# Channel-mix pieces drawn from a queue, centring on ScalarE and a reordered set-up in a fused RWKV-attention and channel-mix kernel

## The chip, the cores and the metric

The kernel runs on one core of one Trainium2 chip. The metric is the device time of one execution in microseconds (us); the median of several runs is quoted. The profile's span leaves out start and end, and is 1.8 to 2.1 us shorter than the time of the same execution in these runs.

## The reference, cut to what matters

Four sequences of 768 positions with 8 heads of 48 go through a linear-attention recurrence, then through a normalised two-layer channel mix with a residual.

```python
for t in range(S):                                   # per batch and head
    y[:, :, t] = r_t @ (state + (u * k_t) ⊗ v_t)
    state = w * state + k_t ⊗ v_t
x  = y as (4, 768, 384)
xn = (x - mean(x)) / sqrt(var(x) + 1e-6) * g_ln
out = x + max(xn @ w_ch1, 0) @ w_ch2                 # 384 -> 1536 -> 384
```

The kernel cuts the 3072 rows into 24 tiles of 128, six a sequence. Within a tile the recurrence becomes matrix products; from tile to tile a state Z is carried.

## The kernel before: the parts that matter

One pass of the main loop, a slot, does the attention of tile s and channel-mix work of earlier tiles. Each engine has its own stream of instructions, in the order of the program. A "piece" is one call of up or down; the bank o is the one buffer into which all down pieces write.

```python
def transposes(i):     # TensorE: 8 transposes into PSUM tr;  ScalarE: trs <- tr;  VectorE: q
def scores(i):         # TensorE: at, s;  VectorE: A, Z;  ScalarE: cc;  GpSimd: Vb
def values(i):
    ...                                             # TensorE: y
    nc.vector.tensor_tensor(out=x[:], in0=y[:, :C], in1=cc_t[i]..., op=ALU.add)
    nc.vector.bn_stats(out=stats[:], in_=x[:])
    nc.vector.bn_aggr(out=mv[:, i % GT, :], in_=stats[:])
    nc.vector.tensor_scalar(out=xn[:], in0=x[:], scalar1=mv[:, i % GT, 0:1],
                            scalar2=None, op0=ALU.subtract)
    ...                                             # every second tile: root on ScalarE, 1/x on VectorE
def ln_transposes(i):  # TensorE: 3 transposes of xn;  ScalarE: xT
def up(g, m):          # TensorE: 6 matmuls;  ScalarE: hT = relu(hp)
def down(i, m):        # TensorE: 4 matmuls into the one bank o;  after the third: VectorE ot, store

for s in range(NT + DN0):        # NT = 24, UP0 = 3, DN0 = 5: fixed delays
    if att: transposes(s)
    ...                          # load(s + 3) on GpSimd's queue
    up_slot(s, 0); down_slot(s, 0)
    if att: scores(s); scale(s + 1)
    up_slot(s, 1)
    ln_transposes(s - 1)
    down_slot(s, 1)
    if att: values(s)
    up_slot(s, 2); down_slot(s, 2)
```

In the set-up, load(0) and tiny transfers are issued ahead of w1 (2.36 MB, three transfers), and ScalarE multiplies w1 by g before it does anything for tile 0.

## Time and profile before

| before | |
|---|---|
| time | 182.42 us, median of 3 (182.04 to 183.57) |
| span, granted clock of the profiled execution (183.27 us) | 181.2 us, 0.991 |
| first x of tiles 1, 10, 23 | 24.42, 77.84, 157.31 us |

x is the first thing VectorE makes of a finished tile, so the starts of x(1), x(10) and x(23) cut the span into head, early slots, late slots and tail. The next lines are the busy times in the last three of these. Columns: stretch, its length, then busy us (and instructions) of TensorE, its weight loads, VectorE, ScalarE, GpSimd, then the clock, the DMA share and GB/s.

```profile
24.42:77.84 53.42, 47.60 (x559) 36.14 (x560) 42.77 (x92) 28.25 (x56) 31.87 (x37) 0.97 1.15 78
77.84:157.31 79.47, 75.41 (x888) 56.11 (x886) 64.21 (x132) 42.58 (x84) 36.46 (x43) 1.00 0.82 71
157.31:181.20 23.89, 17.82 (x127) 11.93 (x124) 5.41 (x11) 6.41 (x12) 0.00 (x0) 1.00 0.14 50
```

The late slots have TensorE busy for 95% (75.41 of 79.47). There is little room there; the head and the tail have more.

### The profile page before, as it was taken

To read this page: it belongs to the slowest core of one execution; us is meant where nothing else is said; L and a number is where in the kernel's file an instruction comes from. 1 tells how busy PE (TensorE), PEld (TensorE's weight loads), DVE (VectorE), ACT (ScalarE), POOL (GpSimd) and SP (SyncE) were. 2 spreads that over 40 slices of the span, in tenths; PEclk is the share of its full clock that TensorE was granted. 3 is DMA by queue.
4 is the path that set the end of the run, shared out by engine and by line. 5 is a ranking of instruction groups with operands and counts; after the bars stand their busy time and mean duration, and the time that the engine had idled before them with its cause. 6 is when DMAs were issued, how large, how long until landed. Compare 5 with 4: busy or idle time off the path is not lost.

```text
span 181.2 us, 4089 instructions
## 1 busy us (share of the span) xinstructions
PE 148.7 (82%) x1646; PEld 110.1 (61%) x1646; DVE 125.7 (69%) x278; ACT 87.3 (48%) x162; POOL 85.9 (47%) x105
## 2 busy tenths in 40 slices
PE   0323558969998999999989999999899999989871
PEld 0212347757676677667666866776677767767640
DVE  0843989876798797878888877878797879621211
ACT  2085262465545453654546455637455555454300
POOL 7946776754773475357536733764471101100000
PEclk9999999988999999999999999999999999999999
DMA  5999999999889968998999799699967110111121
GB/s 21 244 340 141 184 175 79 63 67 65 43 83 97 96 48 79 109 52 84 89 109 56 75 89 111 37 87 99 93 51 77 47 45 0 47 43 45 43 90 43
DMA packets 81971, 15.61 MB, mean 86 GB/s; under 512 B 76960, under 2 KB 81568, under 8 KB 81952
## 3 DMA queue, kind: packets, MB, share of 16 engines
q0 software_dynamic: 76432, 8.26, 80.0%
q1 hardware_dynamic: 5520, 7.09, 11.2%
q8 instruction: 13, 0.21, 0.5%
q14 instruction: 6, 0.05, 0.1%
HBM read 18.88 MB, written 4.72 MB: 130 GB/s over the span
## 4 chain that ended last, share of the span: by engine, by line
PE 47%; DVE 33%; issue 8%; DMA 5%; ACT 4%; SPq 2%; DVEq 0%
PE o L355 20%; PE hp L337 11%; DVE ot L364 8%; DVE stats L302 7%; DVE x L298 7%; DMA w_f<-in_moe_w_ch_dram 5%; PE at L203 5%; DVE xn L308 3%; DVE A L246 3%; DVE mv L306 2%; DVE Z L260 2%; ACT trs L190 2%; PE y L288 2%; PE s L215 2%; PE tr L327 2%
## 5 line engine op out<-in xcount | busy, mean ns | idle before, releaser
L355 PE MATMUL o<-w_sb,hT 128*128 128x384 bf16 x288 | 57.8, 325 | 8.0 <-DVE ot L364 7.7
L337 PE MATMUL hp<-xT,w_sb 128*128 128x256 bf16 x432 | 60.5, 277 | 0.0
L344 ACT ACTIVATE hT<-hp 128x512 bf16<-128x512 f32 x72 | 42.8, 597 | 25.4 <-PE hp L337 25.4
L255 POOL TENSOR_TENSOR Vb<-vv,cc 128x384 bf16<-128x384 bf16 x24 | 19.8, 826 | 66.5 <-ACT cc L253 66.5
L337 PEld LDWEIGHTS <-w_sb 128*128 128x128 bf16 x432 | 38.8, 99 | 5.1
L355 PEld LDWEIGHTS <-hT 128*128 128x128 bf16 x288 | 27.2, 97 | 23.0 <-issue 12.2
L246 DVE TENSOR_TENSOR A<-at,mask 128x512 bf16<-128x512 f32 x48 | 30.9, 685 | 9.5 <-PE at L203 9.2
L190 ACT COPY trs<-tr 128x1024 bf16<-128x1024 bf16 x24 | 24.2, 1006 | 9.1 <-PE tr L188 9.1
L364 DVE SCALAR_TENSOR_TENSOR ot<-o,rs,x 128x384 f32<-128x384 f32 x24 | 14.4, 602 | 15.1 <-PE o L355 15.1
L71 POOL DMA_DIRECT2D rk<-in_k_dram x24 | 22.6, 944 | 0.8 <-POOLq L432 0.8
L72 POOL DMA_DIRECT2D rk<-in_r_dram x24 | 21.3, 889 | 3.0 <-DMA vv<-in_v_dram 3.0
L73 POOL DMA_DIRECT2D vv<-in_v_dram x24 | 21.8, 907 | 0.0
L192 DVE TENSOR_TENSOR q<-trs 128x512 bf16<-128x512 bf16 x24 | 10.2, 425 | 14.9 <-ACT trs L190 14.8
L188 PE MATMUL tr<-ident,sc 128*128 128x128 bf16 x192 | 16.5, 236 | 4.1 <-DVE sc L180 4.1
L188 PEld LDWEIGHTS <-sc 128*128 128x128 bf16 x192 | 13.8, 106 | 7.6 <-DVE sc L180 5.1
L203 PE MATMUL at<-trs 48*128 48x128 bf16 x192 | 10.2, 229 | 8.5 <-ACT trs L190 8.5
L298 DVE TENSOR_TENSOR x<-y,Vb 128x384 f32<-128x384 f32 x24 | 13.3, 554 | 5.1 <-PE y L288 5.1
L203 PEld LDWEIGHTS <-trs 48*128 48x128 bf16 x192 | 5.8, 98 | 15.9 <-ACT trs L190 13.1
L308 DVE TENSOR_SCALAR xn<-x,mv 128x384 bf16<-128x384 f32 x24 | 14.1, 586 | 0.9
L253 ACT COPY cc<-s 128x8 f32<-128x8 f32 x24 | 4.0, 166 | 21.9 <-PE s L235 21.9
L302 DVE BATCH_NORM_STATS2 stats<-x 128x6 f32<-128x384 f32 x24 | 13.5, 560 | 0.8
L180 DVE TENSOR_TENSOR sc<-rk,F 128x768 bf16<-128x768 bf16 x24 | 13.4, 558 | 0.0
(49 smaller groups left out, 127.5 us busy)
## 6 DMA issues: line engine op xcount, KB each, us to landing
out_dram<-ot SPq DMA_DIRECT2D x24, 192.0 KB, 2.6
rk<-in_k_dram POOLq DMA_DIRECT2D x24, 96.0 KB, 3.3
rk<-in_r_dram POOLq DMA_DIRECT2D x24, 96.0 KB, 4.0
vv<-in_v_dram POOLq DMA_DIRECT2D x24, 96.0 KB, 3.9
w_f<-in_moe_w_ch_dram SPq DMA_DIRECT2D x3, 768.0 KB, 7.5
w_sb<-in_moe_w_ch_dram POOLq DMA_DIRECT2D x1, 1152.0 KB, 10.0
w_p<-in_w_dram SPq DMA_DIRECT2D x2, 0.8 KB, 2.0
u_p<-in_u_dram SPq DMA_DIRECT2D x2, 0.8 KB, 3.1
```

Of the source, the lines that this page charges most:

```text
L71: nc.gpsimd.dma_start(out=rk[:, 1], in_=k[b, :, s0 : s0 + L, :].rearrange("h t d -> t h d"))
L73: nc.gpsimd.dma_start(out=vv[:], in_=v[b, :, s0 : s0 + L, :].rearrange("h t d -> t h d"))
L188: nc.tensor.transpose(out=tp[:, j, :], in_=sc[:, j, :], identity=ident[:])
L190: nc.scalar.copy(out=tr[:], in_=tp[:].rearrange("p (a q) t -> p a q t", a=2))
L203: nc.tensor.matmul(out=at[:, par, p, :], lhsT=tr[p0 : p0 + D, 1, p, :], rhs=tr[p0 : p0 + D, 0, p, :], start=True, stop=True,)
L246: nc.vector.tensor_tensor(out=A[:, par], in0=at[:, par], in1=mask[:].unsqueeze(1).to_broadcast([P, HP, P]), op=ALU.mult,)
L298: nc.vector.tensor_tensor(out=x[:], in0=y[:, :C], in1=cc_t[i][:].rearrange("p h d -> p (h d)"), op=ALU.add)
L302: nc.vector.bn_stats(out=stats[:], in_=x[:])
L337: nc.tensor.matmul(out=hp[:, f, :], lhsT=w1_sb[:, kc, fk * P : (fk + 1) * P], rhs=xT_t[g][:, kc, :], start=(kc == 0), stop=(kc == CK - 1),)
L344: nc.scalar.activation(out=hT_t[g][:, 2 * m : 2 * m + 2, :], in_=hp[:], func=ACT.Relu)
L355: nc.tensor.matmul(out=o[:, :C], lhsT=hT_t[g][:, fk, j * P : (j + 1) * P], rhs=w2_sb[:, fk, :], start=(fk == 0), stop=(fk == FK - 1),)
L364: nc.vector.scalar_tensor_tensor(out=ot[:], in0=o[:, :C], scalar=mv_t[g][:, j : j + 1], in1=x_t[i][:], op0=ALU.mult, op1=ALU.add,)
```

## The change

Its intent: no slot without channel-mix work if there is any, and no bare wait for the o bank; less on VectorE; nothing of w1 in tile 0's way on ScalarE. Pieces wait in a queue, and fill(n) emits up to n of them. Centring on ScalarE gives mean - x, so w1 is scaled by -g. The core of the diff:

```diff
-            nc.sync.dma_start(                      # w_p, u_p, and g_sb alike
+            nc.scalar.dma_start(
-    load(0)                                         # now behind make_identity
...                                                  # T chain: F2 in two halves; small constants on GpSimd
-        nc.scalar.activation(out=w1_sb[:, kc, :], in_=w1_f[:, kc, :], func=ACT.Copy, scale=g_sb[...])
+    def scale_w1(kc):
+        nc.gpsimd.tensor_scalar(out=w1_sb[:, kc, :], in0=w1_f[:, kc, :], scalar1=g_neg[...], ...)
...
+    def center(i):                                  # cut out of values(i)
+        nc.vector.bn_aggr(out=mv[:, j, :], in_=st[i][:])
+        nc.scalar.activation(out=xn[:], in_=x_t[i][:], func=ACT.Identity, bias=mv[:, j, 0:1], scale=-1.0)
+        ...                                         # last tile of a group: root, reciprocal
+    group_len = [1, 1] + [GT] * ((NT - 2) // GT)
...
+    def fill(n): ...   # up to n pieces: up and down in turn; a piece is ready one fill after its inputs
+    for s in range(NT):
+        transposes(s)
+        fill(2)
+        scores(s)
+        if s == 0: scale_w1(0)
+        scale(s + 1)
+        if s == 0: load(2); w2
+        load(s + 3)
+        fill(2)
+        if s >= 1: ln_transposes(s - 1); normalised(s - 1)
+        values(s)
+        if s == 0: scale_w1(1); scale_w1(2)
+        fill(2)
+        center(s)
```

More of the change, by code (lines that the diff above doesn't have):

```diff
@@ L87 @@
             )
-    load(0)
     g_sb = const.tile([P, CK], FP32, name="g_sb")
-    nc.sync.dma_start(out=g_sb[:], in_=moe_g_ln.rearrange("(kc p) -> p kc", p=P))
+    nc.scalar.dma_start(out=g_sb[:], in_=moe_g_ln.rearrange("(kc p) -> p kc", p=P))
     w1_f = const.tile([P, CK, F], FP32, name="w1_f")
@@ L101 @@
     make_identity(nc, ident_f[:])
-    ident = const.tile([P, P], BF16, name="ident")
-    nc.vector.tensor_copy(ident[:], ident_f[:])
+    load(0)
     mask = const.tile([P, P], BF16, name="mask")
@@ L115 @@
     load(1)
-    load(2)
+    ident = const.tile([P, P], BF16, name="ident")
+    nc.vector.tensor_copy(ident[:], ident_f[:])
     eps_t = const.tile([P, 1], FP32, name="eps_t")
     nc.vector.memset(eps_t[:], 1e-6)
+    NSC = 3
+    sc_bufs = []
+    for i in range(NSC):
+        t_ = const.tile([P, 2, H, DP], BF16, name=f"sc{i}")
+        nc.vector.memset(t_[:, :, :, D:DP], 0.0)
+        sc_bufs.append(t_)
+    WLZ = const.tile([P, HP, E2], FP32, name="WLZ")
+    nc.vector.memset(WLZ[:], 0.0)
+    uwI = const.tile([P, HP, 2], BF16, name="uwI")
+    nc.vector.memset(uwI[:], 0.0)
     T = const.tile([P, 2 * CK, L + 1], FP32, name="T")
@@ L134 @@
     fps = ps.tile([P, 2, 512], FP32, name="at")
-    for kc in range(CK):
-        nc.tensor.transpose(out=fps[:, 0, kc * P : (kc + 1) * P], in_=T[:, kc, 0:L], identity=ident_f[:])
-    for kc in range(CK):
-        nc.tensor.transpose(out=fps[:, 1, kc * P : (kc + 1) * P], in_=T[:, CK + kc, 1 : L + 1], identity=ident_f[:])
     F2 = const.tile([P, 2, H, D], BF16, name="F2")
-    nc.scalar.copy(out=F2[:], in_=fps[:, :, :C].rearrange("p a (h d) -> p a h d", h=H))
-    wl = const.tile([P, HP], FP32, name="wl")
@@ L144 @@
-    nc.vector.tensor_tensor(out=wl[:], in0=w_p[:], in1=w_p[:], op=ALU.mult)
-    n = 2
-    while n < L:
-        nc.vector.tensor_tensor(out=wl[:], in0=wl[:], in1=wl[:], op=ALU.mult)
-        n *= 2
-    assert n == L
-    WLZ = const.tile([P, HP, E2], FP32, name="WLZ")
-    nc.vector.memset(WLZ[:], 0.0)
-    uwI = const.tile([P, HP, 2], BF16, name="uwI")
-    nc.vector.memset(uwI[:], 0.0)
-    for par in range(2):
-        p0 = par * DP
-        nc.vector.tensor_copy(
-            out=WLZ[p0 : p0 + D, :, par * D : (par + 1) * D],
-            in_=wl[p0 : p0 + D, :].unsqueeze(2).to_broadcast([D, HP, D]),
-        )
-        nc.vector.tensor_tensor(
-            out=uwI[p0 : p0 + D, :, par], in0=u_p[p0 : p0 + D, :], in1=w_p[p0 : p0 + D, :], op=ALU.mult
-        )
@@ L164 @@
-    NSC = 3
-    sc_bufs = []
-    for i in range(NSC):
-        t_ = const.tile([P, 2, H, DP], BF16, name=f"sc{i}")
-        nc.vector.memset(t_[:, :, :, D:DP], 0.0)
-        sc_bufs.append(t_)
-    for kc in range(CK):
-        nc.scalar.activation(
-            out=w1_sb[:, kc, :], in_=w1_f[:, kc, :], func=ACT.Copy, scale=g_sb[:, kc : kc + 1]
+    for a in (1, 0):
+        for kc in range(CK):
+            src = T[:, CK + kc, 1 : L + 1] if a else T[:, kc, 0:L]
+            nc.tensor.transpose(out=fps[:, a, kc * P : (kc + 1) * P], in_=src, identity=ident_f[:])
@@ new lines, with late_constants @@
+    nc.scalar.copy(out=F2[:, 1], in_=fps[:, 1, :C].rearrange("p (h d) -> p h d", h=H))
+    nc.vector.tensor_copy(out=F2[:, 0], in_=fps[:, 0, :C].rearrange("p (h d) -> p h d", h=H))
+    g_neg = const.tile([P, CK], FP32, name="g_neg")
+    def late_constants():
+        wl = const.tile([P, HP], FP32, name="wl")
+        nc.gpsimd.tensor_tensor(out=wl[:], in0=w_p[:], in1=w_p[:], op=ALU.mult)
+        n = 2
+        while n < L:
+            nc.gpsimd.tensor_tensor(out=wl[:], in0=wl[:], in1=wl[:], op=ALU.mult)
+            n *= 2
+        assert n == L
+        for par in range(2):
+            p0 = par * DP
+            nc.gpsimd.tensor_tensor(
+                out=uwI[p0 : p0 + D, :, par], in0=u_p[p0 : p0 + D, :], in1=w_p[p0 : p0 + D, :], op=ALU.mult
+            )
+        for par in range(2):
+            p0 = par * DP
+            nc.gpsimd.tensor_copy(
+                out=WLZ[p0 : p0 + D, :, par * D : (par + 1) * D],
+                in_=wl[p0 : p0 + D, :].unsqueeze(2).to_broadcast([D, HP, D]),
+            )
+        nc.gpsimd.tensor_scalar(
+            out=g_neg[:], in0=g_sb[:], scalar1=-1.0, scalar2=1.0, op0=ALU.mult, op1=ALU.mult
+        )
@@ L174 @@
+    def scale_w1(kc):
+        nc.gpsimd.tensor_scalar(
+            out=w1_sb[:, kc, :],
+            in0=w1_f[:, kc, :],
+            scalar1=g_neg[:, kc : kc + 1],
+            scalar2=1.0,
+            op0=ALU.mult,
+            op1=ALU.mult,
         )
@@ L302, in values @@
         nc.vector.bn_stats(out=stats[:], in_=x[:])
-        if i % GT == 0:
-            mv_t[i // GT] = sm.tile([P, GT, nc.vector.BN_AGGR_DIM], FP32, name="mv", bufs=6)
-        mv = mv_t[i // GT]
-        nc.vector.bn_aggr(out=mv[:, i % GT, :], in_=stats[:])
+        x_t[i] = x
+        st[i] = stats
+    def center(i):
+        g, j = tile_group[i]
+        if j == 0:
+            mv_t[g] = sm.tile([P, GT, nc.vector.BN_AGGR_DIM], FP32, name="mv", bufs=8)
+        mv = mv_t[g]
+        nc.vector.bn_aggr(out=mv[:, j, :], in_=st[i][:])
         xn = sb3.tile([P, C], BF16, name="xn")
-        nc.vector.tensor_scalar(
-            out=xn[:], in0=x[:], scalar1=mv[:, i % GT, 0:1], scalar2=None, op0=ALU.subtract
-        )
-        x_t[i], xn_t[i] = x, xn
-        if i % GT == GT - 1:
-            rs = sm.tile([P, GT], FP32, name="rs", bufs=6)
-            nc.scalar.activation(out=rs[:], in_=mv[:, :, 1], func=ACT.Sqrt, bias=eps_t[:], scale=1.0)
-            nc.vector.reciprocal(out=rs[:], in_=rs[:])
-            mv_t[i // GT] = rs
-    xT_t, hT_t, o_t = {}, {}, {}
+        nc.scalar.activation(
+            out=xn[:], in_=x_t[i][:], func=ACT.Identity, bias=mv[:, j, 0:1], scale=-1.0
+        )
+        xn_t[i] = xn
+        n = group_len[g]
+        if j == n - 1:
+            rs = sm.tile([P, GT], FP32, name="rs", bufs=8)
+            nc.scalar.activation(
+                out=rs[:, :n], in_=mv[:, :n, 1], func=ACT.Sqrt, bias=eps_t[:], scale=1.0
+            )
+            nc.vector.reciprocal(out=rs[:, :n], in_=rs[:, :n])
+            rs_t[g] = rs
+    xT_t, hT_t, o_t, rs_t = {}, {}, {}, {}
+    group_len = [1, 1] + [GT] * ((NT - 2) // GT)
+    assert sum(group_len) == NT
+    tile_group = [(g, j) for g, n in enumerate(group_len) for j in range(n)]
+    group_first = [sum(group_len[:g]) for g in range(len(group_len))]
     def ln_transposes(i):
-        g, j = divmod(i, GT)
+        g, j = tile_group[i]
         if j == 0:
-            xT_t[g] = sb3.tile([P, CK, GW], BF16, name="xT")
+            xT_t[g] = sb3.tile([P, CK, group_len[g] * P], BF16, name="xT")
         tp = ps.tile([P, 2 * HP, P], BF16, name="tr")
@@ L330, in up @@
     def up(g, m):
+        gw = group_len[g] * P
+        nf = 512 // gw
         if m == 0:
-            hT_t[g] = sb2.tile([P, FK, GW], BF16, name="hT")
-        hp = ps_h.tile([P, 2, GW], FP32, name="hp")
-        for f in range(2):
-            fk = 2 * m + f
+            hT_t[g] = sb3.tile([P, FK, gw], BF16, name="hT")
+        hp = ps_h.tile([P, nf, gw], FP32, name="hp")
+        for f in range(nf):
+            fk = nf * m + f
             for kc in range(CK):
@@ L343, in up @@
                 )
-        nc.scalar.activation(out=hT_t[g][:, 2 * m : 2 * m + 2, :], in_=hp[:], func=ACT.Relu)
+        nc.scalar.activation(out=hT_t[g][:, nf * m : nf * (m + 1), :], in_=hp[:], func=ACT.Relu)
     NM = 3
@@ L349, in down @@
     def down(i, m):
-        g, j = divmod(i, GT)
+        g, j = tile_group[i]
         if m == 0:
@@ L366, in down @@
                 in0=o[:, :C],
-                scalar=mv_t[g][:, j : j + 1],
+                scalar=rs_t[g][:, j : j + 1],
                 in1=x_t[i][:],
@@ L373, in down @@
             nc.sync.dma_start(out=out[b, c * L : (c + 1) * L, :], in_=ot[:])
-    AHEAD = 4
-    UP0 = 3
-    DN0 = 5
-    NB = FK // 2
-    def up_slot(s, n_):
-        q_ = s - UP0
-        if q_ < 0:
-            return
-        g, j = divmod(q_, GT)
-        if g < NT // GT:
-            up(g, j * (NB // GT) + n_)
-    def down_slot(s, n_):
-        i_ = s - DN0
-        if 0 <= i_ < NT:
-            down(i_, n_)
-    scale(0)
-    for s in range(NT + DN0):
-        att = s < NT
-        if att:
-            transposes(s)
-        if s + 3 < NT and s + 3 not in rk_t:
-            load(s + 3)
-        if s == 0:
-            nc.gpsimd.dma_start(out=w2_sb[:], in_=w2_src)
-        up_slot(s, 0)
-        down_slot(s, 0)
-        if att:
-            scores(s)
-            if s + 1 < NT:
-                scale(s + 1)
-        up_slot(s, 1)
-        if 0 <= s - 1 < NT:
-            ln_transposes(s - 1)
-        down_slot(s, 1)
-        if att:
-            values(s)
-        up_slot(s, 2)
-        down_slot(s, 2)
+    clock = [0]
@@ new lines, with normalised, fill @@
+    ups, downs = [], []
+    n_up = {}
+    def normalised(i):
+        g, j = tile_group[i]
+        if j == group_len[g] - 1:
+            n_up[g] = FK * group_len[g] * P // 512
+            for m in range(n_up[g]):
+                ups.append((clock[0] + 1, g, m))
+    last_o = [-9]
+    def fill(n):
+        clock[0] += 1
+        for _ in range(n):
+            can_up = ups and ups[0][0] <= clock[0]
+            can_down = downs and downs[0][0] <= clock[0]
+            if can_down and downs[0][2] == 0 and last_o[0] >= clock[0]:
+                can_down = False
+            if can_up and (turn[0] == 0 or not can_down):
+                _, g, m = ups.pop(0)
+                up(g, m)
+                if m == n_up[g] - 1:
+                    for j in range(group_len[g]):
+                        for d in range(NM):
+                            downs.append((clock[0] + 1, group_first[g] + j, d))
+                turn[0] = 1
+            elif can_down:
+                _, i, d = downs.pop(0)
+                down(i, d)
+                if d == NM - 1:
+                    last_o[0] = clock[0]
+                turn[0] = 0
+            else:
+                break
@@ new lines @@
+    turn = [0]
+    scale(0)
+    late_constants()
+    for s in range(NT):
+        transposes(s)
+        fill(2)
+        scores(s)
+        if s == 0:
+            scale_w1(0)
+        if s + 1 < NT:
+            scale(s + 1)
+        if s == 0:
+            load(2)
+            nc.gpsimd.dma_start(out=w2_sb[:], in_=w2_src)
+        if s + 3 < NT:
+            load(s + 3)
+        fill(2)
+        if s >= 1:
+            ln_transposes(s - 1)
+            normalised(s - 1)
+        values(s)
+        if s == 0:
+            scale_w1(1)
+            scale_w1(2)
+        fill(2)
+        center(s)
@@ L421 @@
+    fill(2)
+    ln_transposes(NT - 1)
+    normalised(NT - 1)
+    while ups or downs:
+        fill(2)
 _INS = ['r', 'k', 'v', 'w', 'u', 'moe_g_ln', 'moe_w_ch1', 'moe_w_ch2']
```

## The prediction

> **What bounds the kernel now.** I read the page's busy shares first, then the chain of waits for one steady slot, then the timeline of the head. A "slot" is one pass of the loop: the attention of one 128-row tile plus six pieces of channel mix (an "up" piece is 6 matmuls, a "down" piece 4; 144 pieces in all for 24 tiles).
>
> ```profile
> PE 148.7 (82%) x1646; PEld 110.1 (61%) x1646; DVE 125.7 (69%) x278; ACT 87.3 (48%) x162; POOL 85.9 (47%) x105
> PE   0323558969998999999989999999899999989871
> PE 47%; DVE 33%; issue 8%; DMA 5%; ACT 4%; SPq 2%; DVEq 0%
> ```
>
> TensorE has 82% overall, 9 or more tenths in the middle, little in the first six slices and less at the end: a head (first up at 31.17), a steady part, a tail. Yet a third of the chain is VectorE's. One slot shows why:
>
> ```profile
> 102.39 0.57 DVE x L298
> ...
> 102.99 0.57 DVE stats L302
> ...
> 103.58 0.20 DVE mv L306
> ...
> 104.35 0.61 DVE ot L364
> ...
> 105.00 0.81 PE o L355 x4
> 105.81 0.33 PE at L203 x8
> 106.14 0.27 PE s L215
> 106.41 0.17 PE s L225 x4
> 106.58 0.08 PE s L235 x4
> 106.66 0.68 PE hp L337 x6
> 107.33 0.17 PE tr L327 x3
> 107.50 0.65 PE o L355 x4
> ```
>
> After the last matmul of y, VectorE does x, statistics, mean, centring (0.55) and only then the output ot, which frees the single o bank; TensorE meanwhile does up, down, transposes, up and then waits 0.30 us. From the end of y (102.30) to the first score matmul (105.81) is 3.5 us; from there to the next end of y (108.53) 2.72 us: 6.2 us a slot. x(10) to x(23) took 157.31 - 77.84 = 79.5 us, 6.1 each. TensorE's own work in a full slot is 6 x 0.65 + 0.57 + 0.33 + 0.52 + 0.17 + 0.38 = 5.9, so a perfect queue could save some 0.3 us a slot. In the tail, from x(23) at 157.31 to 181.2, 24 pieces remain, and each finished tile shows a bare ot of about 0.7 us. In the head:
>
> ```profile
> 13.86 1.57 ACT L172 ACTIVATE w_sb<-w_f,g_sb 128x1536 bf16<-128x1536 f32 x1 [0.52 <-DMA w_f<-in_moe_w_ch_dram]
> 15.34 0.99 ACT L190 COPY trs<-tr 128x1024 bf16<-128x1024 bf16 x1
> 17.81 0.83 POOL L255 TENSOR_TENSOR Vb<-vv,cc 128x384 bf16<-128x384 bf16 x1 [0.76 <-ACT cc L253]
> ```
>
> ScalarE scales w1 ahead of the copy trs that the first tile's scores need; its transposes were done at 12.2, so about 3 us are lost. This is what the change aims at.
>
> **What the Trainium skill says.** "ScalarE: Activation LUTs", What ACT_TABLE_LOAD costs: 186 ns + 0.833 ns an element, and 93 ns more for a per-partition operand. hT (512 wide) would be 613; the trace has 597, so it agrees, and the new centring (384 wide, bias by pointer) is estimated at 0.58 us. "GPSIMD Engine Reference", Elementwise side-by-side cycle accounting: two inputs cost about 2.6 cycles an element at 1.2 GHz, so 384 take 0.83 us, and Vb took 0.83; one input costs 1.03 to 1.8 cycles. Scaling 1536 columns of w1 is then estimated at 1.3 to 2.3 us; I take 1.8. "DMA: Bandwidth & Descriptors", Queues, rings and completion order: an engine takes turns between queues packet by packet. The trace agrees and shows the price: with w1's packets of up to 6 KB in flight, the queue of small loads moved about 70 packets in a us (9:10), without them 1490 (15:16), a load being 1024.
>
> **The change, part by part.** The order of the built instruction streams was read along with the diff.
>
> *Head.* w1 is issued from 1.24 instead of 3.71, as the tiny loads move to ScalarE's queue, while load(0) starts about 0.2 us later, behind the identity. Before, k(0) and r(0) just got in ahead of w1 (landed at 5.5 and 6.6), and v(0) waited until 14.0. Now w1 should flow from about 3.4 to 10.2 and hold up r(0) to about 11.7 (estimate: 2000 packets still to go at 1490 a us after w1). The set-up chain is ready at about 8, so the first scaling is at 12 (before: 10.58); but trs(0) no longer waits behind w1's scaling: about 13.6 instead of 15.34, and Vb(0) on GpSimd about 16.1. Then GpSimd's stream is in order: Vb(0) to 16.9, w1 scaling 1.8, load(2) 2.7, w2 1.0, load(3) 2.7, two scalings 3.6, and only then Vb(1): 16.9 + 11.8 = 28.7, Vb(1) ends 29.5. The first up can go at 28.7 (31.17 before), but x(1) comes at 29.6 where it came at 24.42: **+5.2 us** on the attention chain.
>
> *Steady part.* The pieces of each slot come from counting the queue through by hand: from slot 10 on every slot's last pair ends with the third down of a tile. So VectorE's order is x, statistics, ot, mean. ScalarE's order is centring of s, a square root in every second slot, then trs(s+1). All scores of s+1 now hang on ot. From the end of y, taken as 0: x 0.11, statistics 0.71 to 1.27; the down ends at 0.65 + 0.65 = 1.31; ot 1.35 to 1.97; mean to 2.15; centring 2.19 to 2.77; trs to 3.77; scores at 3.8. With the square root (0.29) 4.07. TensorE itself would be there at 1.31 + 0.57 + 1.3 = 3.18, so it waits 0.6 to 0.9 us. With 2.72 as before, a slot is 6.5 or 6.8. Thirteen steps, x(10) to x(23): 7 x 6.52 + 6 x 6.79 - 1.2 for the first and last tiles of a batch, which have fewer score matmuls = 85.2: **+5.7 us** on 79.5. The old wait on the o bank does go, since another piece and the transposes now lie between; it is replaced by a longer one.
>
> *Slots 1 to 10.* By the same chain, step by step, with 2 to 6 pieces each: 6.2, 6.7, 6.15, 6.2, 6.2, 6.5, 5.55, 5.9, 6.5 = 55.9, against 53.4 before: **+2.5 us**. The two one-tile groups let fillers start in slot 1 instead of 3, but the queue is then dry in slot 4 (two pieces), and their ups are 12 matmuls 128 wide (about 0.85 us).
>
> *Tail.* After the last attention 22 pieces remain: 22 x 0.655 + 0.2, about 1.1 of bare ot waits (one whole, two covered by an up), the last ot 0.65 and 3.3 to the end as before: 19.6 instead of 23.9: **-4.3 us**.
>
> Sum: 5.2 + 5.7 + 2.5 - 4.3 = +9.1 us; 181.2 becomes 190 in the profile. Relieving VectorE of 24 x 0.586 = 14 us of centring gains nothing directly.
>
> **Rivals.** (1) *The queue fills TensorE.* If mean and centring get through before the scores' operands are wanted (ScalarE is only 48% busy), a slot falls to about 5.9: 13 x 0.25 = 3 us saved instead of 5.7 lost, and with the tail the time is about 179 to 181. For it: the o wait goes. Against it: the in-order streams named above. (2) *The head gains.* If r(0) slips in before w1 as it did before, everything up to Vb(1) is up to 4 us earlier, and one-input work at 1.03 cycles takes off 1.5 more: about 185 with the steady loss, about 175 if rival 1 holds too. Against it: the 70 packets a us. (3) *GpSimd is slower than I take it*: at the rate of Vb a scaling is 3.3 us, three add 4.5: about 194.
>
> **Range and chances.** My sum is 190. Of its terms the head can err by 5 us, mostly downward, and the steady part by 3 either way; so I put the prediction at 188, with 181 to 194 for 8 in 10. Slower by over 2% starts at 186.1, within my sum's error only if two terms miss together; faster (under 178.8) needs both rivals 1 and 2. Chances: slower 0.63, same 0.23, faster 0.14.
>
> **What would show it.** In the changed kernel's profile: the score matmuls wait on trs in nearly every late slot, and trs is released by the centring, not by TensorE (chain of waits: x, stats, ot, mv, xn, trs, at in a row); TensorE's mean busy share in the late stretch falls from 95% to near 88%; a slot there is 6.5 to 6.8 us. GpSimd shows three scalings of 1.3 to 2.3 us ahead of Vb(1), and x(1) near 29.6. After x(23) there are about 19.6 us. I am wrong if the late slots are at 6.0 or less (rival 1), or x(1) comes before 26 (rival 2).

## The result, and the profile after

The changed kernel takes **197.0 us** (196.0 to 197.46, 4 runs) against 182.38 us (4 runs): slower by 7.8%, ratio 1.0782 with a 95% interval of 1.0718 to 1.0846. Ratios in this document are the mean of one kernel's fast runs over the mean of the other's in the same rounds, so not quite the ratio of the medians.

First the page of the changed kernel: busy time by engine, TensorE's busy tenths in 40 slices, and the shares of the chain that ended last.

```profile
PE 149.4 (77%) x1682; PEld 111.9 (57%) x1682; DVE 113.9 (58%) x245; ACT 96.4 (49%) x184; POOL 93.4 (48%) x120
PE   0323269984996889978978898889788988988981
PE 45%; ACT 22%; DVE 14%; POOL 7%; DMA 5%; issue 4%; POOLq 0%; DVEq 0%
```

VectorE has lost 11.8 us of work and its share of the chain fell from 33% to 14%. But ScalarE, busy for only 49%, now carries 22% of the chain where it carried 4%. TensorE's nines in the middle have become eights. The stretches, with the same columns as before:

```profile
30.08:87.97 57.89, 49.30 (x603) 38.14 (x601) 38.86 (x82) 33.08 (x65) 32.09 (x37) 0.97 1.07 76
87.97:174.23 86.26, 75.63 (x888) 56.84 (x888) 57.35 (x119) 50.30 (x98) 39.11 (x46) 1.00 0.82 69
174.23:195.20 20.97, 15.22 (x109) 10.09 (x106) 4.46 (x9) 6.35 (x13) 0.00 (x0) 0.98 0.14 48
```

The same 888 matmuls are in the late stretch, with nearly the same TensorE time (75.63 us against 75.41); the stretch is 6.8 us longer, so nearly all of that is waiting (88% busy instead of 95%, as predicted). Two late slots in the chain of waits (start, length, what):

```profile
127.89 0.82 PE hp L364 x6
128.71 0.66 PE o L382 x4
...
129.40 0.62 DVE ot L391
130.02 0.10 DVE mv L324
...
130.14 0.61 ACT xn L326
130.75 0.91 ACT trs L203
...
135.63 0.62 DVE ot L391
...
136.37 0.61 ACT xn L326
136.98 0.19 ACT rs L333
137.17 0.91 ACT trs L203
```

After the down, ot, the mean, the centring xn and (in every second slot) the root rs stand in a row ahead of trs, the copy that the next scores need. None of ot, xn and rs is an input of trs: they are only ahead of it in VectorE's and ScalarE's streams. Who waited for whom, first in the kernel before, then in the changed one (total us, times, longest):

```profile
PE at L203 <- ACT trs L190: 8.5, 4, 4.2
PE o L355 <- DVE ot L364: 7.7, 19, 0.7
```

```profile
PE at L216 <- ACT trs L203: 20.5, 23, 3.4
PE hp L364 <- ACT xT L353: 3.0, 11, 0.5
PE o L382 <- DVE ot L391: 0.9, 2, 0.7
```

The wait for the o bank is gone, as intended (7.7 to 0.9 us). The scores' wait for trs has become 20.5 us in 23 of 24 slots, and the first up of a group waits for xT. In the 13 late slots alone the waits for trs are 8.8 us, 0.59 to 0.78 in each, and those for xT 1.7 us in seven; the kernel before has neither there, but 3.9 us for the o bank. The head of the changed kernel:

```profile
13.03 0.56 DVE L193 TENSOR_TENSOR sc<-rk,F 128x768 bf16<-128x768 bf16 x1 [4.31 <-DMA rk<-in_r_dram]
17.19 0.83 POOL L268 TENSOR_TENSOR Vb<-vv,cc 128x384 bf16<-128x384 bf16 x1 [4.42 <-ACT cc L266]
18.00 1.54 POOL L180 TENSOR_SCALAR w_sb<-w_f,g_neg 128x1536 bf16<-128x1536 f32 x1
25.82 3.43 POOL L180 TENSOR_SCALAR w_sb<-w_f,g_neg 128x1536 bf16<-128x1536 f32 x2
30.08 0.56 DVE L311 TENSOR_TENSOR x<-y,Vb 128x384 f32<-128x384 f32 x1 [2.23 <-POOL Vb L268]
```

Tile 0's scaling waits 4.31 us for its load and comes at 13.03 instead of 10.58; x(1) waits for Vb(1), which stands behind the loads and all of w1 on GpSimd.

### The profile page after: what moved, and what is told of

Its sections match the earlier page's. It is cut to its first block, busy times and chain, and to the rows that moved or that the text cites. A ratio compares the mean times of both kernels' runs of the same rounds, so it can differ in the third digit from the quotient of the medians.

```text
span 195.2 us, 4159 instructions
## 1 busy us (share of the span) xinstructions
PE 149.4 (77%) x1682; PEld 111.9 (57%) x1682; DVE 113.9 (58%) x245; ACT 96.4 (49%) x184; POOL 93.4 (48%) x120
## 4 chain that ended last, share of the span: by engine, by line
PE 45%; ACT 22%; DVE 14%; POOL 7%; DMA 5%; issue 4%; POOLq 0%; DVEq 0%
PE o L382 19%; PE hp L364 14%; ACT trs L203 10%; DVE ot L391 7%; ACT xn L326 7%; DMA vv<-in_v_dram 5%; PE at L216 3%; ACT xT L353 2%; POOL w_sb L180 2%; PE s L228 2%; PE tr L352 2%; PE s L238 1%; ACT hT L371 1%; POOL rk L72 1%; POOL rk L71 1%
## 5 line engine op out<-in xcount | busy, mean ns | idle before, releaser
L364 PE MATMUL hp<-xT,w_sb 128*128 128x256 bf16 (+1 forms) x468 | 59.4, 273 | 4.7 <-ACT xT L353 3.0
L382 PE MATMUL o<-w_sb,hT 128*128 128x384 bf16 x288 | 55.9, 325 | 1.2 <-DVE ot L391 0.9
L371 ACT ACTIVATE hT<-hp 128x512 bf16<-128x512 f32 x72 | 41.9, 597 | 28.9 <-PE hp L364 28.6
L364 PEld LDWEIGHTS <-w_sb 128*128 128x128 bf16 x468 | 42.7, 102 | 10.8 <-issue 4.1
L205 DVE TENSOR_TENSOR q<-trs 128x512 bf16<-128x512 bf16 x24 | 11.0, 457 | 29.0 <-ACT trs L203 29.0
L216 PE MATMUL at<-trs 48*128 48x128 bf16 x192 | 10.0, 226 | 20.6 <-ACT trs L203 20.5
L326 ACT ACTIVATE xn<-x,mv 128x384 bf16<-128x384 f32 x24 | 14.7, 614 | 20.6 <-DVE mv L324 20.6
L201 PE MATMUL tr<-ident,sc 128*128 128x128 bf16 x192 | 15.9, 230 | 7.9 <-DVE sc L193 7.9
L353 ACT COPY xT<-tr 128x384 bf16<-128x384 bf16 x24 | 11.5, 478 | 15.5 <-PE tr L352 15.3
L193 DVE TENSOR_TENSOR sc<-rk,F 128x768 bf16<-128x768 bf16 x24 | 15.2, 634 | 4.3 <-DMA rk<-in_r_dram 4.3
```

Of the source, the lines that this page charges most:

```text
L201: nc.tensor.transpose(out=tp[:, j, :], in_=sc[:, j, :], identity=ident[:])
L216: nc.tensor.matmul(out=at[:, par, p, :], lhsT=tr[p0 : p0 + D, 1, p, :], rhs=tr[p0 : p0 + D, 0, p, :], start=True, stop=True,)
L326: nc.scalar.activation(out=xn[:], in_=x_t[i][:], func=ACT.Identity, bias=mv[:, j, 0:1], scale=-1.0)
L364: nc.tensor.matmul(out=hp[:, f, :], lhsT=w1_sb[:, kc, fk * P : (fk + 1) * P], rhs=xT_t[g][:, kc, :], start=(kc == 0), stop=(kc == CK - 1),)
L371: nc.scalar.activation(out=hT_t[g][:, nf * m : nf * (m + 1), :], in_=hp[:], func=ACT.Relu)
L382: nc.tensor.matmul(out=o[:, :C], lhsT=hT_t[g][:, fk, j * P : (j + 1) * P], rhs=w2_sb[:, fk, :], start=(fk == 0), stop=(fk == FK - 1),)
```

## The experiments

All outputs are right. The table has the starts of x and what lies between, from the traces, then the median time and the ratio to the kernel before of the same rounds.

| kernel | x(1) | x(1) to x(10) | x(10) to x(23) | x(23) to end | time | ratio (95%) |
|---|---|---|---|---|---|---|
| before | 24.42 | 53.42 | 79.47 | 23.89 | 182.4 | 1 |
| changed | 30.08 | 57.89 | 86.26 | 20.97 | 197.0 | 1.078 (1.072 to 1.085) |
| e1_mid | 30.02 | 56.49 | 77.78 | 20.51 | 186.56 | 1.023 (1.018 to 1.028) |
| e1_early | 30.12 | 58.48 | 82.32 | 21.48 | 194.11 | 1.063 (1.057 to 1.069) |
| e2_dve | 30.03 | 54.53 | 78.20 | 20.14 | 184.83 | 1.012 (1.006 to 1.017) |
| e3_before_act | 24.94 | 58.82 | 82.88 | 24.76 | 193.48 | 1.061 (1.055 to 1.066) |
| e4_loads | 28.04 | 56.99 | 86.23 | 21.04 | 194.27 | 1.066 (1.062 to 1.071) |
| e5_pairs | 30.06 | 57.44 | 77.78 | 20.32 | 187.43 | 1.027 (1.023 to 1.031) |
| e6_w1act | 27.45 | 56.85 | 77.76 | 20.44 | 184.29 | 1.011 (1.005 to 1.016) |
| e7_lntr | 30.02 | 55.60 | 76.01 | 20.47 | 184.48 | 1.011 (1.007 to 1.015) |
| e8_head | 23.39 | 57.58 | 75.99 | 20.34 | 179.11 | 0.979 (0.975 to 0.983) |
| e9_best | 23.21 | 57.53 | 74.90 | 19.16 | 176.42 | 0.963 (0.959 to 0.967) |
| e10_best_dve | 23.11 | 51.68 | 76.76 | 18.85 | 172.43 | 0.942 (0.939 to 0.945) |

The stretches of e2_dve are those of e2_look, the same kernel. e2_look is a single run, so its state is unknown; its time (184.74 us) and clock (0.986) are like those of e2_dve's fast runs (184.33 to 184.87 us, 0.985 to 0.987).

### The place of the centring: e1_mid and e1_early

e1_mid leaves TensorE's stream alone and moves the small steps of center(s) (the mean, xn and, at the end of a group, the root with its reciprocal) between the two pieces of the third fill; e1_early moves them ahead of both.

```diff
-        fill(2)
-        center(s)
+        fill(2, lambda: center(s))      # e1_mid: center(s) is emitted after the fill's first piece
```

```diff
-        fill(2)
         center(s)
+        fill(2)                         # e1_early
```

> The changed kernel with centring (mean, xn, root) emitted between the two pieces of the third fill instead of after it; the pieces and their order on TensorE stay. Theory (chain ot, mean, xn, trs, at in two in-order streams): trs no longer waits on ot or on the up's ReLU; slots x(10) to x(23) fall from 86.3 us to about 79 to 80, slots before them by 2 to 3 us; time about 187 to 188. Rival A (the loss is the queue itself: the first up of a group waiting for xT, one-tile groups): at most 1 us gained, 196. Rival B (any centring on ScalarE costs it): no gain, 196 to 197.

> The changed kernel with centring emitted before the third fill. Then xn stands ahead of the ReLU of the third fill's up on ScalarE, and trs stands behind both. Theory (the whole of ScalarE's order counts, not only ot): xn done 2.15 us after y, ReLU 2.75, with the root 2.95, trs 3.7 to 3.9: slots of about 6.5, x(10) to x(23) about 84, time about 194. Rival (only the mean's place behind ot counts): as e1_mid, 187 to 188.

e1_mid took 186.56 us (187 to 188 expected) and e1_early 194.11 us (about 194 expected). The late slots of e1_mid fell from 86.26 to 77.78 us, further than the 79 to 80 expected and under the 79.47 of the kernel before; slots 1 to 10 fell by 1.4 us, less than the 2 to 3 expected. Part of its chain:

```profile
123.42 0.65 PE o L382 x4
124.07 0.45 PE tr L201 x8
124.51 0.66 PE hp L364 x6
125.17 0.65 PE o L382 x4
125.82 0.33 PE at L216 x8
```

After the down, TensorE goes through transposes, up and down to the scores without a wait: ot, xn and trs of that slot were done beside it. In the slots with a root the scores still wait for trs, but only 0.20 us, in six of the 13 late slots. In e1_early:

```profile
121.57 0.61 ACT xn L326
122.18 0.19 ACT rs L333
122.37 0.48 ACT hT L371
122.85 0.91 ACT trs L203
```

Here the mean is no longer behind ot, and yet the slot stays long (82.32 us): xn, which waits for the mean, now also holds up the up's ReLU hT, and trs stands behind all three. So both streams count, and the rival that blamed only the place behind ot fell. Moving these steps alone is worth 10.4 us (197.0 to 186.56), with the same work on every engine (busy 96.4 and 96.3 us on ScalarE, 113.9 and 114.6 on VectorE): the order, not the load, cost that time. What e1_mid still loses against the kernel before is 5.6 us up to x(1) and 3.1 from there to x(10), less 1.7 in the late slots and 3.4 in the tail.

### The engine of the centring: e2_dve, e2_look and e3_before_act

e2_dve keeps the changed kernel's late place but makes xn on VectorE; e3_before_act does that one part of the change alone in the kernel before.

```diff
-        nc.scalar.activation(out=xn[:], in_=x_t[i][:], func=ACT.Identity, bias=mv[:, j, 0:1], scale=-1.0)
+        nc.vector.tensor_scalar(out=xn[:], in0=x_t[i][:], scalar1=mv[:, j, 0:1], scalar2=-1.0,
+                                op0=ALU.subtract, op1=ALU.mult)       # e2_dve, e2_look
```

```diff
-        nc.vector.tensor_scalar(out=xn[:], in0=x[:], scalar1=mv[:, i % GT, 0:1], ...)
+        nc.scalar.activation(out=xn[:], in_=x[:], func=ACT.Identity, bias=mv[:, i % GT, 0:1], scale=-1.0)
                                                     # e3_before_act; w1 is scaled by -g
```

> The changed kernel with xn made on VectorE, at the same late place. Theory: VectorE gets 14 us busier, yet trs hangs on nothing of VectorE but the root in odd slots; x(10) to x(23) about 80, time about 188. Rival (relief of VectorE is worth something in itself): slower than the changed kernel, 198 to 205.

> The kernel of e2 again, for a profile in the fast state. Theory: x(10) to x(23) about 79 us, and no score matmul waits on a trs that waited for VectorE.

> The kernel before with one part of the change alone: xn made on ScalarE in its old place (w1 scaled by minus g so that the sign comes out). Theory: the o bank's wait of 0.3 us goes, but xn now stands ahead of the ReLU and of trs on ScalarE, scores start about 3.8 to 4.0 us after y instead of 3.5: slots 6.4 to 6.6 instead of 6.15, time about 188 to 190 against 182.4. Rival (TensorE only waits for the o bank; relief of VectorE pays): 176 to 178.

e2_dve took 184.83 us (about 188 expected): giving VectorE back the centring made the changed kernel 12 us faster. In e2_look, x(10) to x(23) took 78.20 us, as expected. Its second expectation failed: in six late slots the scores wait 0.27 us for trs, which stands behind the root, which waits for VectorE's mean. e3_before_act took 193.48 us, so this one part, done alone, costs 11 us, more than the 188 to 190 expected. Its late slots are as predicted (82.88 / 13 = 6.4 us each), but the o bank's wait did not go: it is 4.1 us there, in six slots, against 3.9 in eleven of the kernel before. Its early slots lost 5.4 us, of which 3.8 lie between x(1) and x(3), where there are few pieces or none to cover the chain from y over xn to the next scores. 1.28 us of that is the load of ScalarE's table for the first root: it starts at 23.84 in the kernel before, beside VectorE's x, and here stands between xn and trs (26.95). The rival, that relief of VectorE pays, is refuted for these two kernels; where the chain is covered, relief does pay a little (1.9 us in the late slots, e9_best against e10_best_dve below).

### The head: e4_loads and e6_w1act

e4_loads puts load(0) ahead of the identity again and the tiny transfers back on the sync queue ahead of w1. e6_w1act, on top of e1_mid, makes the scalings of w1 on ScalarE at the same places of the program.

```diff
+    load(0)                                          # e4_loads: before g_sb and w1
-            nc.scalar.dma_start(                     # w_p, u_p, g_sb
+            nc.sync.dma_start(
-    load(0)                                          # was behind make_identity
```

```diff
-        nc.gpsimd.tensor_scalar(out=w1_sb[:, kc, :], in0=w1_f[:, kc, :], scalar1=g_neg[...], ...)
+        nc.scalar.activation(out=w1_sb[:, kc, :], in_=w1_f[:, kc, :], func=ACT.Copy, scale=g_neg[...])
```

> The changed kernel with the old order of the first transfers: load(0) ahead of the identity, the tiny loads back on the sync queue ahead of w1. Theory (w1's packets starve the small loads; GpSimd's stream to Vb(1) starts when tile 0's loads have landed): k(0), r(0) land by 7 instead of 13, sc(0) at about 8.8; v(0) still waits behind w1 to about 14, so Vb(0) comes at about 15.2 instead of 17.2, x(1) at 28.0 instead of 30.1, time 194.5 to 195.5. Rival A (the transfers are not what holds tile 0): unchanged, 197. Rival B (the whole lead of r(0) carries through): x(1) at 25.6, 192.5.

> As e1_mid, but the three scalings of w1 made on ScalarE at the same places of the program (after cc of tile 0). Theory (GpSimd's in-order stream holds Vb(1) and with it x(1)): Vb(1) waits only for its scores, x(1) at about 27 instead of 30, time about 183.5. Rival (the head does not reach the end, TensorE takes up the slack later): 186 to 187.

e4_loads has x(1) at 28.04 and takes 194.27 us, 2.7 less than the changed kernel: what the new order of the first transfers costs. sc(0) came at 10.97, not at 8.8, as the identity is now later, and the rest of VectorE's set-up with it. Vb(0) came at 15.14 as expected, but by luck: v(0), which was to set that time, had landed at 13.60, and the late sc(0) set it. What w1's hold on the small loads costs is therefore not measured apart from the identity's place. In the changed kernel the queue of the small loads moved 21 packets in the us from 6 to 7, beside w1, and 1405 from 11 to 12. e6_w1act has x(1) at 27.45 and takes 184.29 us, 2.3 under e1_mid: GpSimd's scaling held up Vb(1). In both, the lead in x(1) carried to the end.

### The queue and the groups: e5_pairs and e7_lntr

Both build on e1_mid. e5_pairs has groups of two tiles only; e7_lntr emits the transposes of xn ahead of the second fill, so that xT is there when the third fill's first up wants it.

```diff
-    group_len = [1, 1] + [GT] * ((NT - 2) // GT)
+    group_len = [GT] * (NT // GT)                    # e5_pairs
```

```diff
+        if s >= 1: ln_transposes(s - 1)              # e7_lntr
         fill(2)
-        if s >= 1: ln_transposes(s - 1)
```

> As e1_mid (186.6), but all groups of two tiles. Theory: the queue leaves the same 20 pieces after the last tile, so one-tile groups bring nothing at the end and cost 36 narrow matmuls twice; slots 1 to 5 get shorter, 184 to 185.5. Rival (early fillers are worth their place): 188 to 190.

> As e1_mid, but the transposes of xn are emitted before the second fill instead of after it, so that xT is copied before the third fill's first up wants it. Theory: TensorE's wait for xT, 0.2 to 0.5 us and a restart of 0.15 in eleven slots, goes: 182.5 to 183.5. Rival (those waits only stand in for another wait behind them): 185.5 to 187.

e5_pairs took 187.43 us, 0.9 more than e1_mid, and the intervals of the two ratios overlap. The gain of 1 to 2.5 us that I expected did not come; whether the one-tile groups gain a little is not shown. The difference in the traces lies between x(1) and x(10). e7_lntr took 184.48 us, 2.1 less than e1_mid and between the two expectations. The wait of an up for xT disappears from the late stretch (it was 1.7 us there in e1_mid), but the six waits for trs in the slots with a root stay (1.2 us there in both).

### A version that beats both: e8_head, e9_best and e10_best_dve

e8_head joins e1_mid, e7_lntr and e6_w1act, issues load(0) and load(1) ahead of w1, loads the table with the root at the start and makes the third scaling one slot later. e9_best moves the root behind trs and gives two of the last tiles the bank of s for their output. e10_best_dve is e9_best with xn on VectorE.

```diff
+    nc.gpsimd.memset(w1_f[:, :, 0:1], 0.0)           # e8_head: behind load(1); w1's transfers wait for it
+    for kc in range(CK):
+        nc.sync.dma_start(out=w1_f[:, kc, :], in_=w1_src[:, kc, :])
+    nc.scalar.activation(out=root0[:], in_=eps_t[:], func=ACT.Sqrt)
```

```diff
         transposes(s)
+        if s >= 1: root(s - 1)                       # e9_best: cut out of center(s - 1)
-            o_t[i] = ps.tile([P, 512], FP32, name="o")
+            o_t[i] = ps.tile([P, 512], FP32, name="s" if i in (NT - 3, NT - 1) else "o")
```

> Towards a kernel that beats both: e7 (184.5) with w1 scaled on ScalarE as in e6, tile 0's and 1's loads issued ahead of w1 (w1 made to wait for them), and the table with the root loaded at the start. Theory (w1's packets and GpSimd's stream set the head): all small loads of tile 0 land by 7, x(0) at about 14 to 15, x(1) at 21 to 22 against 30; the lead carries to the end: 175.5 to 177.5. Rival (another limit stands close behind, the landing of load(2), load(3) or w2): x(1) early but x(3) or x(4) late, 179 to 182.

> e8 with the root moved behind trs on ScalarE, and the outputs of the last tiles in a second PSUM bank. Theory: odd slots lose 0.2 us of ScalarE ahead of trs (1 to 1.5 us over the loop), the tail loses two to three bare waits of 0.7 us and a restart each (about 2 us): 3 us under e8, 172.5 to 174.5. Rival (the tail is held by ReLU and hT, not by the bank): 1 us under e8.

> e9 with xn made on VectorE in the same place. With trs no longer behind xn, TensorE should be the bound in every slot. Theory: where the chain is already hidden (slot 5.75 to 5.85) the engine of centring no longer matters: within 1.5 us of e9. Rival (VectorE, freed or not, is the next bound): 2 to 5 us over e9.

e8_head took 179.11 us, which is in its rival's range: x(1) came at 23.39 (21 to 22 expected), and from x(1) to x(2) it took 8.3 us, where e1_mid took 6.6. The trace has three waits around it: the first up waits 1.1 us for xT and starts only at 23.25, the first down waits 0.5 us for w2 (to 29.55), and tile 3's scaling, which stands ahead of x(2) on VectorE, waits 1.1 us for load(3), issued behind w2 (to 31.19).

e9_best took 176.42 us, 2.7 under e8_head where about 3 was expected; the time misses 172.5 to 174.5, as e8_head had missed its own. Its two changes are not tested apart; in the traces the late slots give 1.1 us and the tail 1.2. e10_best_dve took **172.43 us**, 5.8% under the kernel before (0.942, 0.939 to 0.945) and 12.5% under the changed one (172.43 / 197.0). I had expected the engine of the centring to matter no longer; it was worth 4 us. All of it and more lies in the early slots (51.68 against 57.53 us), where few pieces cover the chain: the scores wait for trs 2.4 us there, against 6.2 in e9_best. In the late slots VectorE costs 1.9 us, because xn stands ahead of ot again and the old wait for the o bank is back (2.2 us in six slots; e9_best has no such wait there).

## Why the prediction was right or wrong, point by point

The direction, the cause and each stretch's sign were right; the time was wrong. 197.0 us lies outside 181 to 194: the loss is 14.6 us where 5.6 was forecast (188.0 against 182.42).

- **Head, +5.2 us.** Measured +5.7: x(1) at 30.08, predicted 29.6. sc(0) came at 13.03 instead of 12; GpSimd's scaling, 1.54 us and then 1.7 each instead of 1.8, took part of that back. Rival 2 did not come; e4_loads and e6_w1act show that both causes named, the order of the first transfers and GpSimd's stream, were at work.
- **Late slots, +5.7 us.** Measured +6.8 (86.26 us; 85.2 predicted). The row ot, mean, xn, trs, at was there as written: TensorE waited 0.59 to 0.78 us in every slot (0.6 to 0.9 predicted); e1_mid takes most of this away, and 8.5 us with it. In the slots with a root the scores started 3.84 us after the end of y, sooner than the 4.07 predicted. In those without one they started after 4.01 to 4.19 instead of 3.8. What the term had left out there: the first up of a group waits for xT (1.7 us in seven slots), and the first piece after a wait shows its whole 0.82 us in the chain, while a piece that follows another adds 0.66. The way from the scores to the next y took 34.8 us in all, 0.6 more than predicted (13 x 2.72 - 1.2).
- **Slots 1 to 10, +2.5 us.** Measured +4.5. The steps I put at 6.2, 6.5 and 5.55 us (1 to 2, 6 to 7, 7 to 8) took 6.91, 6.90 and 6.27. The chain shows something else left out in each: ReLUs of the first group ahead of xn (31.88 to 32.47), as its ups had waited for the last scaling of w1 until 29.31; the wait of an up for xT; and ot ahead of x on VectorE. No experiment takes these apart. The last two in the chain:

```profile
62.27 0.49 ACT xT L353
...
75.24 0.61 DVE ot L391
75.85 0.47 DVE x L311
```

- **Tail, -4.3 us.** Measured -2.9: 20.97 us, not 19.6. The last xn, root, two ReLUs and xT stand in a row on ScalarE ahead of the last group's first up (176.21 to 178.40), which I had counted as free; TensorE's wait for this xT is 0.5 us. From the last ot to the end it took 3.6 us, not 3.3. The rest of the 1.4 us is not taken apart. The 24 pieces that I read in the tail of the kernel before are 26 in its trace (60 up and 64 down matmuls after the last y); the sum does not use that number.
- **The step that failed is the sizing.** My sum gave a span of 190.3; the span is 195.2. All four terms were too favourable, by 0.5 (head), 1.1 (late), 2.0 (slots 1 to 10: 57.9 us, not 55.9) and 1.4 us (tail: 21.0, not 19.6), because I counted only the waits I had named. The paragraph on range and chances then went further the wrong way: it held that the head errs "mostly downward", took 2 us off the sum, took it as a time although it was a span (added to the time of 182.42, the four terms give 191.5), and put the top of the range only 4 us above the sum.
- **Rival 1, the queue fills TensorE,** was refuted for the changed kernel (6.6 us a late slot) and is what e1_mid and e7_lntr then reach (6.0 and 5.8, against its 5.9). Rival 3 fell, as GpSimd was faster than I took it.
- "Relieving VectorE gains nothing directly" held, and was too mild: e2_dve and e3_before_act show that the move to ScalarE was a loss in itself, in its place in both kernels.
- The centring was put at 0.58 us; the formula that I quoted from "ScalarE: Activation LUTs", What ACT_TABLE_LOAD costs, gives 0.60 (0.186 + 0.093 + 384 x 0.000833), and it took 0.61.

What stays open: e8_head's 8.3 us from x(1) to x(2) is explained only in part. The gains of the experiments overlap, so they are no exact split of the 14.6 us.

## What to carry to other kernels

Where an engine runs its stream in order, read what stands ahead of the instruction that the bound engine waits for, not only its inputs: here ScalarE, 49% busy, set the pace because the copy for the next scores stood behind a centring that stood behind an output. Moving work to a less busy engine can lengthen the chain it is put into. Here all four terms of a sum that counted only named waits erred to the same side; leave the range open on that side.

## What the Trainium skill lacked or had wrong

- "GPSIMD Engine Reference", Elementwise side-by-side cycle accounting, has no row for a one-input multiply by a per-partition scalar with a cast. Here 1536 fp32 columns to bf16 took 1.54 us and later 1.7, 1.2 to 1.3 cycles an element at the page's 1.2 GHz, between its 1.03 for a loop body of few operations and its 1.8 for a tight unrolled loop, which the prediction took as the cost with one input.
- "SBUF — State Buffer", Who interferes with whom, says that a VectorE instruction with two SBUF inputs contends with a GpSimd one that reads SBUF. The runs agree, so nothing is wrong here, and they add a size: the multiply sc(1) took 1.77 us beside GpSimd's scaling of w1 (18.00 to 19.54), and 0.55 in e6_w1act, where ScalarE did that work.
- "DMA: Bandwidth & Descriptors", Queues, rings and completion order, gives the turn by packets but no figure for what small packets lose. In the changed kernel the three queues moved 64 packets each from 7 to 8 us and again from 8 to 9, as the profile counts them; w1's were 0.33 and 0.36 MB, those of the small loads 0.01 MB. The small loads got 21 to 79 packets in a us beside w1, and 1405 without it, so that r(0), issued at 2.51, took 10.4 us to land.
- No page that I used warns that an instruction's place in a stream can cost more than its engine's load; the figure here is the 10.4 us between the changed kernel and e1_mid.
